# Two-token rows of q and k, Sinkhorn routing on POOL, and weight scales from sums of absolutes, in a one-core attention and expert kernel

## The chip, the cores and the metric

The kernel runs on one core of one Trainium2 chip. The metric is device microseconds of one execution. The engines are PE (matrix products), ACT, DVE and POOL (elementwise work), and SP, which here only issues DMA transfers. Each engine takes its instructions strictly in the order in which they are written for it, and waits where an operand isn't ready.

## The reference

Chunked attention with 8 memory keys is followed by a dense mixture of 8 experts, whose gates are found with 8 Sinkhorn iterations over all 3,072 tokens:

```python
# attention: q, k, v are (4, 8 heads, 768, 64); chunk 32, 16 tokens of left and 8 of right context
k_full = concatenate([mem_k, k_ctx]); v_full = concatenate([mem_v, v_ctx])
scores = scale * q_c @ k_full.T
a = exp(scores - scores.max(-1)); a = a / (a.sum(-1) + 1e-9)
x = a @ v_full                              # reshaped to (3072, 512)
# experts: w_gate (512, 8), w1 (8, 512, 1024), w2 (8, 1024, 512)
logits = x @ w_gate; P = exp(logits - logits.max())
for _ in range(8):
    P /= P.sum(1, keepdims=True) + 1e-9
    P /= P.sum(0, keepdims=True) + 1e-9
    P *= N / E
out = sum(P[:, e:e+1] * (maximum(x @ w1[e], 0) @ w2[e]) for e in range(8))
```

## The kernel before

**Tiling.** Attention goes by 24 blocks of 128 tokens (4 batches of 6). For a block, q and k are loaded with a token on each partition (128 x 8 heads x 64), each of their four 128x128 pieces is turned by PE (`transposed`, tiles tq and tk; for the extra context keys tx), ACT copies the results out (qT, kC), PE makes the scores (sp), DVE takes the row maximum off (sm, s), ACT takes the exponential in place, PE turns it (ta), ACT copies it (at), PE multiplies with v (xp), and DVE divides by the row sums into a tile xq (`share`) and turns it into xg, the layout that the experts read (`turn_out`). xq shares its one buffer with at.

The experts go by 48 units: 8 experts x 6 groups of 512 tokens. Every f32 operand is split into two f16 parts (ACT writes the high part, DVE the low one), and a product is three f16 products. Later units use Strassen's scheme of seven half-size products (px, py, pz for the hidden layer; yx, yy, yz for the output); the very first unit uses plain products (pp, yp). Before a split, a power of two is found for the whole tensor: a maximum of absolutes per partition (`most`, into mxs, or vmax for v, which bounds x), one small maximum over those (most_of), a PE transpose to one row (row_x, row_w), a maximum of that row, a PE product with ones that spreads it (sp_x, sp_w), and a reciprocal (sx, sw).

**Stages.** The attention of later blocks runs among the products of expert 0 (to some 294 us); from some 375 us the rest is a steady row of units. In the prologue PE can do only attention of the first blocks; what it lacks is filled with dummy products called warm (`fill`). The first real product is pp_0_0_0, which needs x of blocks 0 and 1 and the first piece of w1.

**What sets the order.** One planner, `Plan.run`, simulates all engines with a cost for each task and due times (`prio`), and writes the order of each engine's instructions from that; START, TURN, UNIT, AHEAD, BLOCKS, VALUES, FIRST and `needed` feed the due times. Buffers are rings: a task that names a buffer waits for all users of the slot's earlier content. DMA transfers are issued by SP in one stream, except v of the first blocks, which ACT issues.

**Routing.** `routing` runs once, after the last attention block: in each of 8 iterations DVE makes row sums, divides, and makes column sums over its 24 token groups, PE adds over partitions with a product with ones (cp), and DVE scales the columns. Its result, pscale, is first read by an ACT line (`fetch_acc`).

Of the kernel before, what the change touches and what calls it, by code (L numbers as in the profile page):

```python
# [233 lines left out]
def tile_chunked_attn_sinkhorn_moe(  # L234
# [58 lines left out]
    small = ctx.enter_context(tc.tile_pool(name="small", bufs=1))  # L293
    xpool = ctx.enter_context(tc.tile_pool(name="xpool", bufs=1))
# [51 lines left out]
    START, TURN, UNIT, AHEAD = 28.2, 63.0, 36.7, 50.0  # L346
# [340 lines left out]
    def plain1(fp, st, ld, prio):  # L687

        o = operands("w1", [P, 2, 7, 2, P], f"w1_0_{fp}")
# [56 lines left out]
    extra = {}
# [86 lines left out]

    def load_block(n):
# [4 lines left out]
        qt = buf("q", att, [P, H, D], F32, f"q_{n}")  # L839
        kt = buf("k", att, [P, H, D], F32, f"k_{n}")  # L840

        def go_k():
            if blk == 0:
# [5 lines left out]
        lq = add(  # L849
            "SP", 1, lambda: nc.sync.dma_start(qt.t, rows(q, b, t0, QB)), (), at, [qt], dma=1.55  # L850
        )
        lk = add("SP", 2 if blk == 0 else 1, go_k, (), at + 0.1, [kt], dma=1.55)
# [142 lines left out]
    def transposed(n):  # L995
# [10 lines left out]
        def go_q():  # L1006
            for i in range(HP):
                nc.tensor.transpose(tq.t[:, i], flat(qt, i), ident)  # L1008

        def go_k():  # L1010
            for i in range(HP):
# [19 lines left out]
        t = add("PE", 0.5, go_q, [lq], at, [qt, qT], takes=tq)  # L1031
# [11 lines left out]
        t = add("PE", 0.5, go_k, [lk], at, [kt, kC], takes=tk)  # L1043
# [70 lines left out]
    def values(n, s, made):  # L1114
# [31 lines left out]
        t = add("PE", 0.5, go_t, [made], at, [s, aT], takes=tp)  # L1146
# [3 lines left out]
        xq = buf("at", att, [P, CB, KT, CH], F32, f"xq_{n}")  # L1150
        rec = buf("sm", att, [P, H], F32, f"rec_{n}")

        def share():
# [4 lines left out]
            for a in range(2):  # L1158
                nc.vector.tensor_tensor(
                    xq.t[:, :, :, a * CH // 2 : (a + 1) * CH // 2],  # L1160
# [5 lines left out]
        t = add("DVE", 1.25, share, [t], at + 2, [xq, rec], frees=xp)  # L1166
# [11 lines left out]
        def turn_out():  # L1178
            nc.vector.transpose(
                gt.t[:, :, o : o + QB].rearrange("p k (c q) -> p k c q", c=CB),  # L1180
                xq.t.rearrange("p c k f -> p k c f"),
            )

        t = add("DVE", 0.73, turn_out, [t], at + 2, [xq, gt])
# [272 lines left out]

    def routing(deps):
# [4 lines left out]
        urgent = begin(LATE) + 58.5  # L1463
# [27 lines left out]
        def rows(it):  # L1491
            def go():
                rs = small.tile([P, NT], F32, tag="rs", bufs=1, name=f"rs_{it}")
                nc.vector.tensor_reduce(rs, lg, axis=AX.X, op=ALU.add)
                nc.vector.tensor_scalar_add(rs, rs, 1e-9)
                nc.vector.reciprocal(rs, rs)
                nc.vector.tensor_tensor(
                    lg, lg, rs[:, :, None].broadcast_to([P, NT, E]), op=ALU.mult
                )
# [7 lines left out]
        def columns(it, cp):  # L1507
            def go():
                cr = small.tile([P, E], F32, tag="cr", bufs=1, name=f"cr_{it}")
                nc.vector.tensor_scalar_add(cr, cp.t, 1e-9)  # L1510
                nc.vector.reciprocal(cr, cr)
# [811 lines left out]
```

## Time and profile before

| | us |
|---|---|
| median of 3 runs (range) | 1913.08 (1911.89 to 1914.97) |
| the profiled execution: time, span | 1913.3, 1911.5 |
| PE busy, DVE, ACT, POOL | 1898.8, 1468.1, 1022.5, 503.0 |
| granted TensorE clock, mean | 0.999 |

Of PE's busy time, 26.5 us are the 183 dummy products of line 427. Times in the views of the trace count from the first instruction of the span. In a row of the timeline stand the start, the time of the instruction or of the group (a PE group's last matmul is drawn longer than the distance to the next, so start-to-start distances are the better price), the engine, the line, the operation, and in brackets the idle time before it with what ended it. One plain fp32 product shows as two records; a transpose shows as one.

### The profile page before, as it was taken

Reading aid. Unit: us, or ns where it says so; the run is one execution under the profiler, and the core shown is the slowest. Engines: PE = TensorE matmul, PEld = TensorE weight load, DVE = VectorE, ACT = ScalarE, POOL = GpSimd, SP = SyncE. Lnnn points to the kernel's source line nnn. Section 1 sums busy time; section 2 is a strip of 40 time slices with the busy share of each in tenths; the row PEclk is TensorE's granted clock in tenths of the full one; section 3 lists DMA queues with packets and bytes.
Section 4 is the critical chain, followed back from the end, with each engine's and each line's share of the span. In section 5 each row is a group of like instructions: output and inputs, shape, how many; then the busy total and the mean of one; then the engine's idle time right before and its main releaser. Section 6 shows DMA issues by size and latency. Waiting matters only on the chain.

```text
span 1911.5 us, 47024 instructions
## 1 busy us (share of the span) xinstructions
PE 1898.8 (99%) x19535; PEld 1634.8 (86%) x19535; DVE 1468.1 (77%) x2456; ACT 1022.5 (53%) x1999; POOL 503.0 (26%) x541
## 2 busy tenths in 40 slices
PE   8999999999999999999999999999999999999999
PEld 7777676788888888888888888888888888888888
DVE  5887679878589867898668875898678885786565
ACT  4665555556465545546446544655555563564453
POOL 1210012514134211522224231342124232332112
PEclk9999999999999999999999999999999999999999
DMA  8787653543324432264224433245313632222321
GB/s 198 189 219 182 160 173 133 169 169 106 126 80 160 150 134 77 90 217 165 84 91 154 165 119 114 84 155 188 127 45 111 247 112 97 98 84 83 127 84 67
DMA packets 212998, 254.81 MB, mean 133 GB/s; under 512 B 112240, under 2 KB 146480, under 8 KB 208432
## 3 DMA queue, kind: packets, MB, share of 16 engines
q1 hardware_dynamic: 210660, 251.21, 40.4%
q8 instruction: 153, 2.51, 0.6%
q10 hardware_dynamic: 2124, 0.59, 0.2%
q14 instruction: 61, 0.50, 0.1%
HBM read 187.84 MB, written 63.44 MB: 131 GB/s over the span
## 4 chain that ended last, share of the span: by engine, by line
PE 97%; DVE 2%; SPq 0%; ACT 0%; issue 0%; DMA 0%; POOL 0%; DVEq 0%; POOLq 0%
PE px L1593 26%; PE yx L1593 23%; PE pz L1593 13%; PE yz L1593 11%; PE py L1593 6%; PE yp L2121 6%; PE yy L1593 6%; PE pp L2040 1%; PE xp L1138 1%; PE sp L1071 1%; PE warm L427 1%; DVE w L521 1%; PE ta L1128 1%; PE tk L1012 1%; PE tq L1008 1%; SPq L923 0%
## 5 line engine op out<-in xcount | busy, mean ns | idle before, releaser
L1593 PEld LDWEIGHTS <-w 128*128 128x128 f16 x7896 | 771.2, 98 | 94.4 <-issue 2.8
L1593 PEld LDWEIGHTS <-h 128*128 128x128 f16 x7056 | 690.4, 98 | 81.1 <-issue 0.9
L1593 PE MATMUL px<-x,w 128*128 128x256 f16 x4512 | 547.8, 273 | 1.5 <-DVE c L1662 1.0
L1926 POOL TENSOR_TENSOR acc<-acc,y 128x256 f32<-128x256 f32 x252 | 262.4, 1049 | 881.1 <-ACT y L1901 868.5
L1593 PE MATMUL yx<-w,h 128*128 128x256 f16 x4032 | 467.9, 273 | 0.5 <-DVE acc L1936 0.5
L1652 ACT ACTIVATE q<-px 128x256 f32<-128x256 f32 x376 | 143.1, 382 | 289.6 <-PE px L1593 285.1
L1593 PE MATMUL pz<-x,w 128*128 128x256 f16 x2256 | 278.1, 273 | 0.0
L1593 PE MATMUL yz<-w,h 128*128 128x256 f16 x2016 | 233.8, 273 | 0.0
L1821 DVE TENSOR_TENSOR h<-ss,h 128x1024 f16<-128x1024 f32 x168 | 217.6, 1298 | 3.3 <-ACT h L1797 3.3
L1772 ACT ACTIVATE h<-c 128x768 f16<-128x768 f32 x168 | 140.7, 838 | 112.2 <-DVE c L1662 112.2
L1797 ACT CAST h<-ss 128x1024 f16<-128x1024 f32 x168 | 174.2, 1040 | 39.5 <-DVE ss L1761 39.5
L1761 DVE SCALAR_TENSOR_TENSOR ss<-c,ss 128x256 f32<-128x256 f32 x336 | 176.6, 525 | 8.6
L1805 DVE SCALAR_TENSOR_TENSOR h<-c,h 128x768 f16<-128x768 f32 x168 | 168.7, 1007 | 9.2 <-ACT h L1772 9.1
L1662 DVE SCALAR_TENSOR_TENSOR c<-px,q 128x256 f32<-128x256 f32 x188 | 77.8, 421 | 94.8 <-PE px L1593 85.6
L1901 ACT ACTIVATE y<-yx,pscale 128x256 f32<-128x256 f32 x168 | 79.6, 474 | 120.5 <-PE yx L1593 116.5
L1593 PE MATMUL py<-x,w 128*128 128x256 f16 x1128 | 139.0, 273 | 0.0
L2121 PE MATMUL yp<-w,h 128*128 128x512 f16 x576 | 132.0, 379 | 0.9 <-DVE h L2082 0.9
L1761 DVE SCALAR_TENSOR_TENSOR ss<-c,h 128x512 f32<-128x512 f32 x168 | 125.6, 748 | 1.9 <-ACT h L1749 1.9
L1662 DVE SCALAR_TENSOR_TENSOR c<-py,q 128x256 f32<-128x256 f32 x188 | 78.5, 421 | 62.0 <-PE py L1593 58.7
L1593 PE MATMUL yy<-w,h 128*128 128x256 f16 x1008 | 116.9, 273 | 0.0
L2121 PEld LDWEIGHTS <-h 128*128 128x128 f16 x576 | 55.3, 99 | 60.0 <-DVE h L2082 1.4
L513 ACT ACTIVATE w<-ws,sw 128x1024 f16<-128x1024 f32 (+1 forms) x64 | 69.5, 1090 | 65.7 <-POOL ws L601 65.6
(155 smaller groups left out, 1739.6 us busy)
## 6 DMA issues: line engine op xcount, KB each, us to landing
x<-xkeep SPq DMA_DIRECT2D x28, 1792.0 KB
akeep<-acc SPq DMA_DIRECT2D x168, 256.0 KB
acc<-akeep SPq DMA_DIRECT2D x168, 256.0 KB
w1f<-in_moe_w_dram SPq DMA_DIRECT2D x36, 512.0 KB
w2f<-in_moe_w_dram SPq DMA_DIRECT2D x32, 512.0 KB
w1fm<-in_moe_w_dram SPq DMA_DIRECT2D x28, 512.0 KB
w2fm<-in_moe_w_dram SPq DMA_DIRECT2D x28, 512.0 KB
xkeep<-x SPq DMA_DIRECT2D x6, 1792.0 KB
```

Of the source, the lines that this page charges most:

```text
L513: lambda: nc.scalar.activation(dst(0), src(), AF.Copy, scale=s),
L1593: nc.tensor.matmul(dst.t, a, b, start=(not more and n == 0), stop=(n == end), skip_group_check=more,)
L1652: lambda: nc.scalar.activation(t.t, src.t, AF.Copy, scale=DOWN),
L1662: lambda: nc.vector.scalar_tensor_tensor(c.t[:, o], src.t, DOWN, q.t, op0=ALU.mult, op1=ALU.add),
L1761: lambda: nc.vector.scalar_tensor_tensor(dst(), src(), 0.0, other(), op0=ALU.max, op1=op),
L1772: lambda: nc.scalar.activation(h.t[:, 0, 0:3], c.t, AF.Relu),
L1797: lambda: nc.scalar.copy(h.t[:, 0, 3:7], ss.t),
L1805: lambda: nc.vector.scalar_tensor_tensor(h.t[:, 1, 0:3].rearrange("p a n -> p (a n)"), c.t.rearrange("p a n -> p (a n)"), 0.0, h.t[:, 0, 0 ...
L1821: lambda: spare.tensor_tensor(h.t[:, 1, 3:7], ss.t, h.t[:, 0, 3:7], op=ALU.subtract),
L1901: (lambda: nc.scalar.activation(t.t, src.t, AF.Copy, scale=f))
L1926: lambda: nc.gpsimd.tensor_tensor(acc.t[:, cols], acc.t[:, cols], q.t, op=ALU.add),
L2121: nc.tensor.matmul(py.t, hf.t[:, hl, where[fh], o : o + P], room(fp, WIDE * wl + DM * fh, WIDE * wl + DM * (fh + 1)), start=(fp == 0 and i ...
```

## The change

1. **Two-token rows.** For blocks 0 to 5 (`TWOS`), q and k are loaded with two consecutive tokens on one partition row: 64 partitions x 8 heads x 128 elements, so a contiguous run has 512 bytes, not 256. The two buffers of the ring are the two halves of the partitions (0 to 63, 64 to 127) of one tile. PE turns such a tile with 16 plain fp32 products of 64x64 with the identity instead of 4 transposes of 128x128. Later blocks are as before; block 6 waits until block 5 has been turned.
2. **Weight scales from sums.** For w1 of expert 0 and for w1 and w2 of experts 1 to 7 (60 pieces), ACT takes the absolute with a running sum over the partition (`total`, `total_m`) instead of DVE's maximum. w2 of expert 0 keeps the maximum.
3. **Divided results** go into s, the buffer of the softmax weights, instead of xq; at is alone in its buffer.
4. **Fewer waits on PE**: the tasks that turn q, k and s no longer name the buffer into which ACT copies their result.
5. **Routing on POOL**: row sums, the two multiplications and the column sums over groups are POOL additions and products in halves (10 instructions an iteration, into a new tile, tree); DVE adds 1e-9, takes reciprocals and scales 24 or 8 numbers; PE's cp stays. Its due time is earlier, and that of its DVE and PE parts far earlier.
6. **Numbers** of the order: START, TURN, AHEAD, BLOCKS, VALUES, FIRST, `needed`, and the due times of weights, maxima and `rebuild`.

```diff
-    START, TURN, UNIT, AHEAD = 28.2, 63.0, 36.7, 50.0
+    START, TURN, UNIT, AHEAD = 27.4, 66.0, 36.7, 49.9
...
+    def total(fp, which, st, deps, prio, junk):
+        def go():
+            flat = st.t.rearrange("p a k f -> p (a k f)" if which == 1 else "p a d -> p (a d)")
+            nc.scalar.activation(
+                junk.t[:, :, 4:6].rearrange("p j o k f -> p j (o k f)"),
+                flat.rearrange("p (j f) -> p j f", j=2),
+                AF.Abs,
+                accum_out=mxs[:, 0, which - 1, fp : fp + 1],
+            )
+        return add("ACT", 1.15, go, deps, prio, [st, junk])
+    def total_m(e, fp, which, st, deps, prio):
+        def go():
+            flat = st.t.rearrange("p a k f -> p (a k f)" if which == 1 else "p a d -> p (a d)")
+            nc.scalar.activation(
+                flat, flat, AF.Abs, accum_out=mxs[:, e, which - 1, fp : fp + 1]
+            )
+        return add("ACT", 1.1, go, deps, prio, [st])
...
-                found.append(most(e, fp, which, st, [ld], prio))
+                found.append(total_m(e, fp, which, st, [ld], prio))
...
+    TWOS = 6
+    HB = QB // 2
+    qk_rooms = {kind: att.tile([P, 2 * H * D], F32, name=f"{kind}_room") for kind in "qk"}
...
+    def twos(src, b, t, m):
+        return src[b, :, t : t + m].rearrange("h (p a) d -> p h (a d)", a=2)
+    def two_turns(to, t, n):
+        r = slice(n % 2 * HB, (n % 2 + 1) * HB)
+        for i in range(HP):
+            for a in range(2):
+                for par in range(2):
+                    nc.tensor.matmul(
+                        to.t[par * D : (par + 1) * D, i, a::2],
+                        t.t[:, 2 * i + par, a * D : (a + 1) * D],
+                        ident[r, r],
+                        start=True,
+                        stop=True,
+                    )
...
-        t = add("PE", 0.5, go_q, [lq], at, [qt, qT], takes=tq)
+        t = done_q[n] = add("PE", 0.85 if n < TWOS else 0.5, go_q, [lq], at, [qt], takes=tq)
...
-        t = add("PE", 0.5, go_t, [made], at, [s, aT], takes=tp)
+        t = add("PE", 0.5, go_t, [made], at, [s], takes=tp)
...
-        xq = buf("at", att, [P, CB, KT, CH], F32, f"xq_{n}")
+        def turning():
+            return s.t.rearrange("p h k -> p (h k)").rearrange(
+                "p (c k f) -> p c k f", c=CB, k=KT
+            )
...
-        t = add("DVE", 1.25, share, [t], at + 2, [xq, rec], frees=xp)
+        t = add("DVE", 1.25, share, [t], at + 2, [s, rec], frees=xp)
...
-        urgent = begin(LATE) + 58.5
+        urgent = begin(LATE) + 30.0
...
+        def row_sums():
+            two = tree[0][:, 0 : NT * E // 2].rearrange("p (t e) -> p t e", t=NT)
+            one = tree[0][:, NT * E // 2 :].rearrange("p (t e) -> p t e", t=NT)
+            plus(two, lg[:, :, 0 : E // 2], lg[:, :, E // 2 :])
+            plus(one, two[:, :, 0:2], two[:, :, 2:4])
+            plus(rs, one[:, :, 0], one[:, :, 1])
...
         for it in range(8):
-            t = add("DVE", 1.8, rows(it), [t], urgent)
+            t = add("POOL", 1.0, row_sums, [t, opened[0]], urgent)
+            t = add("DVE", 0.5, row_parts, [t], urgent - 300.0)
+            t = add("POOL", 2.1, over_rows, [t], urgent)
...
-            t = add("DVE", 0.8, columns(it, cp), [t], urgent, frees=cp)
+            t = add("DVE", 0.5, column_parts(cp), [t], urgent - 300.0, frees=cp)
+            t = add("POOL", 0.8, over_columns, [t], urgent)
...
-                weights(0, fp, 1, begin(1) - 16.8 + 2.0 * fp)
-            maxima(1, begin(3) + 15.8)
+                weights(0, fp, 1, begin(1) - 10.0 + 2.0 * fp)
+            maxima(1, begin(3) + 0.0)
...
-                weights(e + 1, fp, 1, begin(n + 1) - 8.9 + (0, 0, 20.0, 24.0)[fp])
+                weights(e + 1, fp, 1, begin(n + 1) - -12.9 + (0, 0, 20.0, 24.0)[fp])
```

**DVE, from block 1's scores to the first split of a weight.** Before (mxs: maxima of w1's four pieces; rec, xq, xg: the division and turn of block 1):

```order
L1091 TENSOR_TENSOR s_474<-sp_431,sm_471 128x2x4x64
L976 TENSOR_REDUCE vmax<-v_pair 128x1
L557 TENSOR_REDUCE mxs<-w1f_0_286 128x1
L557 TENSOR_REDUCE mxs<-w1f_1_289 128x1
L1156 TENSOR_SCALAR rec_555<-xp_517 128x8
L1157 RECIPROCAL rec_555<-rec_555 128x8
L1159 TENSOR_TENSOR xq_558<-xp_517,rec_555 128x16x16 x2
L1179 STREAM_TRANSPOSE xg_466<-xq_558 128x4x128
L557 TENSOR_REDUCE mxs<-w1f_2_339 128x1
L557 TENSOR_REDUCE mxs<-w1f_3_363 128x1
L445 TENSOR_REDUCE most_of<-vmax 128x1
L445 TENSOR_REDUCE most_of<-mxs 128x1
```

With the change, from x's scale on:

```order
L458 RECIPROCAL sx<-ux 128x1
L1233 TENSOR_SCALAR rec_588<-xp_552 128x8
L1234 RECIPROCAL rec_588<-rec_588 128x8
L1236 TENSOR_TENSOR s_497<-xp_552,rec_588 128x16x16 x2
L1256 STREAM_TRANSPOSE xg_528<-s_497 128x4x128
L446 TENSOR_REDUCE most_of<-mxs 128x1
L522 SCALAR_TENSOR_TENSOR x_640<-xg_528,sx,x_640 128x512 x2
L503 TENSOR_REDUCE most_of<-row_w_0_649 1x1
...
L458 RECIPROCAL sw<-uw 128x1
L1044 TENSOR_REDUCE vmax<-w_0_2_349 128x1
L522 SCALAR_TENSOR_TENSOR w_0_0_499<-w1f_0_294,sw,w_0_0_499 128x512 x2
```

The four maxima of w1 are gone, x's scale is done before block 1's division, and x's low parts are made before w1's scale; vmax of block 2 (from w_0_2, its buffer) still stands between w1's scale and the first weight split.

**ACT at the same place.** With the change, where before the copy of block 1's at was followed at once by qT of block 2:

```order
L587 ACTIVATE w_0_0_499,mxs<-w1f_0_294 128x2x512
L1182 ACTIVATE s_497<-s_497 128x512
L587 ACTIVATE w_0_1_530,mxs<-w1f_1_298 128x2x512
L1219 COPY at_539<-ta_523 128x512
L587 ACTIVATE w_0_2_585,mxs<-w1f_2_346 128x2x512
L587 ACTIVATE w_0_3_598,mxs<-w1f_3_380 128x2x512
L514 ACTIVATE x_640<-xg_528,sx 128x512 x2
L1108 ACTIVATE qT_668<-tq_623 128x512
```

The four sums stand among block 1's exponential and copy. On PE, 177 of the 183 dummy products stand ahead of the first real product before, and all of 109 now; block 2's scores and the turns of block 3's q and k, which followed the first real product's first half, now stand ahead of it.

**POOL in routing**, one iteration and its neighbours (ws_1_0: the sums of expert 1's first weight piece for Strassen's scheme; tree, row_parts, column_parts: routing):

```order
L625 TENSOR_TENSOR ws_1_0_5553<-w1f_0_5490 128x256
L1609 TENSOR_TENSOR lg<-lg,column_parts 128x192
L1574 TENSOR_TENSOR tree<-lg 128x96
L1574 TENSOR_TENSOR tree<-tree 128x48
L1574 TENSOR_TENSOR row_parts<-tree 128x24
L625 TENSOR_TENSOR ws_1_0_5553<-ws_1_0_5553,w1f_0_5490 128x256
L1588 TENSOR_TENSOR lg<-lg,row_parts 128x192
L1574 TENSOR_TENSOR tree<-lg 128x96
L1574 TENSOR_TENSOR tree<-tree 128x48
L1574 TENSOR_TENSOR tree<-tree 128x24
L1574 TENSOR_TENSOR tree<-tree 128x8 x2
L625 TENSOR_TENSOR ws_1_0_5553<-w1f_0_5490 128x256
```

Before, POOL had only such weight and x sums there, and none of routing. Now 21 of them (of x's last group and of expert 1's weights) stand among the 80 instructions of the 8 iterations.

More of the change, by code (lines that the diff above doesn't have):

```diff
@@ L832, in flat, with qk_buf, make @@
         return t.t[r, 2 * i : 2 * i + 2].rearrange("p h d -> p (h d)")
+    TWOS = 6
+    HB = QB // 2
+    qk_rooms = {kind: att.tile([P, 2 * H * D], F32, name=f"{kind}_room") for kind in "qk"}
+    def qk_buf(kind, n):
+        room_ = qk_rooms[kind]
+        def make(i):
+            if n < TWOS:
+                return room_[i * HB : (i + 1) * HB].rearrange("p (h d) -> p h d", h=H)
+            return room_[:, i * H * D : (i + 1) * H * D].rearrange("p (h d) -> p h d", h=H)
+        return rings[kind].take(make)
+    def twos(src, b, t, m):
[12 more added lines that the diff above has]
+                    )
     def load_block(n):
@@ L838, in load_block, with go_q @@
         at = needed(n) - 25.0 if n >= BU else BLOCKS[n]
-        qt = buf("q", att, [P, H, D], F32, f"q_{n}")
-        kt = buf("k", att, [P, H, D], F32, f"k_{n}")
-        def go_k():
-            if blk == 0:
+        qt = qk_buf("q", n)
+        kt = qk_buf("k", n)
+        out_q = [done_q[n - 1]] if n == TWOS else []
+        out_k = [done_k[n - 1]] if n == TWOS else []
+        cost = 1.1 if n < TWOS else 1.55
+        def go_q():
+            nc.sync.dma_start(qt.t, twos(q, b, t0, QB) if n < TWOS else rows(q, b, t0, QB))
+        def go_k():
+            if n < TWOS:
+                if blk == 0:
+                    nc.sync.dma_start(kt.t[0 : LC // 2], twos(k, b, 0, LC))
+                    nc.sync.dma_start(kt.t[LC // 2 :], twos(k, b, 0, P - LC))
+                else:
+                    nc.sync.dma_start(kt.t, twos(k, b, t0 - LC, P))
+            elif blk == 0:
                 nc.sync.dma_start(kt.t[0:LC], rows(k, b, 0, LC))
@@ L847, in go_k @@
                 nc.sync.dma_start(kt.t, rows(k, b, t0 - LC, P))
[L849 to L852, printed above, removed]
+        lq = add("SP", 1, go_q, out_q, at, [qt], dma=cost)
+        lk = add("SP", 2 if blk == 0 else 1, go_k, out_k, at + 0.1, [kt], dma=cost)
         state[n] = (qt, kt, lq, lk)
@@ L1456, in attention @@
         values(*pend.pop(0))
+    halves_at = small.tile([P, 2, NT], F32, name="row_parts")
+    cols_at = small.tile([P, E], F32, name="column_parts")
     def routing(deps):
@@ L1507, in columns @@
[L1507 to L1511, printed above, removed]
-                nc.vector.scalar_tensor_tensor(
-                    lg,
-                    lg,
-                    float(N) / float(E),
-                    cr[:, None, :].broadcast_to([P, NT, E]),
-                    op0=ALU.mult,
-                    op1=ALU.mult,
-                )
-            return go
+        rs, rr = halves_at[:, 0], halves_at[:, 1]
@@ L1527, in routing @@
                 "PE",
-                0.4,
-                lambda it=it, cp=cp: nc.tensor.matmul(
-                    cp.t, ones, box[it], start=True, stop=True
+                0.2,
+                lambda cp=cp: nc.tensor.matmul(
+                    cp.t,
+                    ones,
+                    tree[0][:, 4 * E : 5 * E],
+                    start=True,
+                    stop=True,
                 ),
                 [t],
-                urgent,
+                urgent - 300.0,
                 takes=cp,
             )
-            t = add("DVE", 0.8, columns(it, cp), [t], urgent, frees=cp)
+            t = add("DVE", 0.5, column_parts(cp), [t], urgent - 300.0, frees=cp)
+            t = add("POOL", 0.8, over_columns, [t], urgent)
         def finish():
@@ L2168, in fetch_first @@
             staged.append((st, ld))
-            found.append(most(0, fp, which, st, [ld], at - 12.0))
+            if which == 1:
+                found.append(total(fp, which, st, [ld], at - 12.0, first1[fp]))
+            else:
+                found.append(most(0, fp, which, st, [ld], at - 12.0))
         scale_w(0, which, found, at - 10.0, "att")
         return staged
+    first1 = [operands("w1", [P, 2, 7, 2, P], f"w1_0_{fp}") for fp in range(FP)]
     first2.extend(operands("w2", [P, 2, 7, DH], f"w2_0_{fp}") for fp in range(FP))
-    for fp, s in enumerate(fetch_first(1, START)):
+    for fp, s in enumerate(fetch_first(1, START + 2.3)):
         plain1(fp, *s, START - 6.0 + 2.0 * fp)
```

69 lines of the change are left out of this document (45 added, 24 removed).

## The prediction

> **What bounds the kernel now.** First the chain of waits of the page, then the busy time by stage:
>
> ```profile
> PE 97%; DVE 2%; SPq 0%; ACT 0%; issue 0%; DMA 0%; POOL 0%; DVEq 0%; POOLq 0%
> ...
> 0.00:38.40 38.40, 33.59 (x480) 26.73 (x481) 18.32 (x40) 13.45 (x26) 4.96 (x12) 0.96 0.80 175
> 38.40:72.00 33.60, 31.86 (x608) 23.71 (x606) 32.29 (x57) 24.72 (x49) 7.32 (x6) 1.00 0.73 179
> ...
> 375.00:1911.00 1536.00, 1531.67 (x14018) 1371.25 (x14015) 1177.82 (x1891) 812.02 (x1581) 432.44 (x453) 1.00 0.35 123
> ```
>
> PE is the bound: after the length of a window stands its busy time, 1531.67 of 1536 in the steady stage. So only two things can move the end: work added to or taken from PE, and PE time that does no work of the problem. The second lies at the start, where dummies fill PE (the same windows for the dummies alone, then the first real product in the timeline):
>
> ```profile
> 0.00:38.50 38.50, 25.70 (x177) 0.96 0.80 175
> 38.50:294.00 255.50, 0.85 (x7) 1.00 0.70 186
> ...
> 38.37 0.82 PE L2040 MATMUL pp<-x,w 128*128 128x256 f16 x6
> ```
>
> Until the first real product at 38.4 us PE has 25.7 us of dummies. Its other large waits, up to 72 us and then behind (in all, times, longest):
>
> ```profile
> PE xp L1138 <- DMA k<-in_k_dram: 1.5, 1, 1.5
> PE yp L2121 <- DVE h L2082: 0.9, 1, 0.9
> PE tk L1012 <- DVE lg L1425: 0.7, 1, 0.7
> ...
> PE px L1593 <- DVE c L1662: 1.0, 3, 0.5
> ```
>
> Behind 38.4 us PE idles 1.7 (33.60 - 31.86) and, from 375 us on, 4.3 us in all. What holds the first product is DVE's chain, told by these rows:
>
> ```profile
> 21.75 0.69 DVE L1091 TENSOR_TENSOR s<-sp,sm 128x512 f32<-128x512 f32 x1
> 23.49 2.33 DVE L557 TENSOR_REDUCE mxs<-w1f 128x1 f32<-128x1024 f32 x2
> 27.10 0.17 DVE L1156 TENSOR_SCALAR rec<-xp 128x8 f32<-128x8 f32 x1 [1.27 <-PE xp L1138]
> 29.03 2.30 DVE L557 TENSOR_REDUCE mxs<-w1f 128x1 f32<-128x1024 f32 x2
> 31.37 0.16 DVE L445 TENSOR_REDUCE most_of<-mxs 128x1 f32<-128x4 f32 x1
> 34.83 0.17 DVE L457 RECIPROCAL sw<-uw 128x1 f32<-128x1 f32 x1
> 35.24 1.22 DVE L976 TENSOR_REDUCE vmax<-w 128x1 f32<-128x1024 f32 x1 [0.24 <-DMA w<-in_v_dram]
> 36.38 1.41 DVE L521 SCALAR_TENSOR_TENSOR x<-xg,sx,x 128x512 f16<-128x512 f32 x2
> 37.70 5.38 DVE L521 SCALAR_TENSOR_TENSOR w<-w1f,sw,w 128x512 f16<-128x512 f32 x8
> ```
>
> Block 1's division (27.10) separates w1's maxima; the last pair ends at 31.3, w1's scale at 35.0, and x's low parts and block 2's vmax (2.6 us together) still stand ahead of the first weight split.
>
> **The change part by part.** *The first product.* The transfers that the new order leans on:
>
> ```profile
> 18.66 0.55 SPq L850 DMA_DIRECT2D q<-in_q_dram  x1
> 19.31 3.53 SPq L847 DMA_DIRECT2D k<-in_k_dram  x1
> 22.93 7.54 SPq L923 DMA_DIRECT2D w<-in_v_dram  x8
> 30.57 0.39 SPq L850 DMA_DIRECT2D q<-in_q_dram  x1
> 31.06 0.54 SPq L847 DMA_DIRECT2D k<-in_k_dram  x1
> ...
> DMA packets 2047, 0.52 MB, mean 258 GB/s; under 512 B 2047, under 2 KB 2047, under 8 KB 2047
> ...
> DMA packets 638, 0.63 MB, mean 315 GB/s; under 512 B 23, under 2 KB 638, under 8 KB 638
> ...
> 22.48 0.63 ACT L1110 ACTIVATE s<-s 128x512 f32<-128x512 f32 x1 [1.97 <-DVE s L1091]
> 34.40 1.33 ACT L513 ACTIVATE x<-xg,sx 128x512 f16<-128x512 f32 x2 [0.19 <-DVE sx L457]
> ```
>
> The packets are those of 12 to 14 us (256-byte q, k) and of 20 to 22 us (1 KB, w1). Runs of 512 bytes have no row; between the two rates 256 KB take 0.83 to 1.02 us, so 0.1 is saved a transfer by bytes. By count it is more: SP is held for 3.5 us at k of block 2 and block 2's v pieces take 7.5 us for 8 issues, with 2,048 packets of q and k ahead; half as many should free about 2 us of it. I take v of block 2 landed by 29 to 30, k of block 3 by some 32.
>
> The DVE chain, step by step. Block 1's maximum and subtraction now precede block 0's division, so s ends near 20.8 (22.4 before); exponential, ta, its copy and xp follow as before with 4.6 us from s to the division (27.10 - 22.44), less 1.5 of a wait for a transfer inside: division at 24.0 to 24.6, turn out (1.9 us, 27.10 to 29.03) at 26.5. ACT's sums have no row; the nearest, ACT's 128x1024 cast, is
>
> ```profile
> L1797 ACT CAST h<-ss 128x1024 f16<-128x1024 f32 x168 | 174.2, 1040 | 39.5 <-DVE ss L1761 39.5
> ```
>
> 1.04 us, so 1.1 each (lower 1.0; upper 1.4, two 0.7 us halves, as ACT's 128x512 rows have it). The last two fall at 24 to 26.6, behind at and w1's landing. Then most_of at 26.8; x's parts on ACT 26.6 to 28.0 and DVE to 28.7; row_w meanwhile on PE; its maximum, the power of two, sp_w and sw: now 3.6 (31.37 to 35.0) with x's own scale and a wait for row_x inside, a third of it without them, 1.2: 29.9; vmax 1.2: 31.1; first split 0.7: 31.8. PE's list, however, has sp of block 2 (0.8), three dummies and both turns of block 3 ahead of the product, some 3.1 us behind sw: 33.0, and 33.3 with k of block 3 landing at 32. Product at 33.3 instead of 38.4: **-5.1**. Bounds: 31.8 (DVE alone) to 36.5 (below).
>
> *PE work brought forward and made dearer:*
>
> ```profile
> 55.66 0.86 PE L1071 MATMUL sp<-kC,qT 64*32 64x64 f32 x64
> 48.23 0.60 PE L1012 MATMUL tk<-ident,k 128*128 128x128 f32 x4
> 48.67 0.82 PE L2040 MATMUL pp<-x,w 128*128 128x256 f16 x6
> 63.43 1.08 PE L1394 MATMUL lp<-xg,gate 128*32 128x128 f32 x32
> 64.44 1.47 PE L2121 MATMUL yp<-w,h 128*128 128x512 f16 x6
> ```
>
> Block 2's scores (0.79) and block 3's two turns (0.44 each, 48.23 to 48.67) no longer follow the first product: **-1.7**. The 16 products of 64x64 have no row. Nearest is lp: 16 plain fp32 products with 128 columns moved and a quarter of the array's columns used take 1.01, 63 ns each; half the columns moved and twice the array's columns make the same, so 1.0 us for 16. Below, sp's 25 ns a product: 16 in 0.4, no dearer than now. Above, if the halves of the array don't overlap: 2.0. I take 1.0, +0.56 a turn. Blocks 0 to 3 pay it in dummy time (that is in the 33.3); blocks 4 and 5, four turns, pay it on PE: **+2.2** (0 to +6.2).
>
> *Sums of later weights.* DVE loses 60 times 1.2 us, ACT gains 60 times 1.1. Both hide behind PE, DVE being the fuller (1177.8 against 812.0 of 1536). Cover gone would cost at most what a read of PSUM delayed by 1.1 us costs at a piece, and px waits for DVE's c already for 1.0 in all; I take **-0.5** for all waits behind 38.4 us (from -2.7 to +3). The first output product waits for the low part of h, that is for DVE:
>
> ```profile
> 67.86 1.21 DVE L2082 SCALAR_TENSOR_TENSOR h<-c,h 128x512 f16<-128x512 f32 x1
> ```
>
> From the first weight split (37.70) to its end are 31.4 us, DVE without pause. The new order puts 1.4 us more ahead of it (block 4's maximum and subtraction): from a split at 32.6, 65.4, 3.7 earlier than now. PE has by then six more products of yp and one more turn behind it (1.3 + 0.4), so the gain by this chain is 5.4, against 5.1 - 2.2 + 1.7 = 4.6 by PE's own list: neither chain takes back what the other gives.
>
> *Routing.*
>
> ```profile
> L1497 DVE TENSOR_TENSOR lg<-lg,rs x8: 357/358/511, 300.7 to 331.8; 128x192 f32<-128x192 f32 x8
> ...
> 300.27 0.73 POOL L601 TENSOR_TENSOR ws<-w1f 128x256 f32<-128x256 f32 x1 [5.74 <-DMA w1f<-in_moe_w_dram]
> 340.42 1.17 POOL L601 TENSOR_TENSOR ws<-w1f,ws 128x256 f32<-128x256 f32 x1
> ...
> 373.08 0.70 ACT L1852 ACTIVATE acc<-acc,pscale 128x512 f32<-128x512 f32 x1
> ```
>
> POOL takes 0.73 for 256 elements; with 0.1 of fixed time assumed, one iteration's ten (two of 192, two of 96, two of 48, two of 24, two of 8) are 2.8 us. DVE's five small ones, at the 0.17 of the row at 27.10, are 0.9, cp and the hand-overs 0.5. The 21 weight and x sums among them are 18 at 0.85. All told 8 x 4.2 + 18 = 52 us; it ends before 350, and its reader is at 373. cp stands in PE's list with 60 to 72 products between two, at 109 ns (1531.67 by 14018, above) 59 us for the eight: no wait, **0**. The buffer of s for xq and the dropped names: **0**, hidden in the order above.
>
> Sum: 1913.3 (the profiled execution, 0.2 above the median) - 5.1 - 1.7 + 2.2 - 0.5 = 1908.2; by the median **1908.0**.
>
> **Rivals.** *A, rows of two tokens don't come sooner.* A transfer that fills 64 partitions may be no faster than one of 128. Then SP's stops stay, k of block 3 is issued until 31.6, it and q are 512 KB or 2.0 us at 258 GB/s, I allow as much again for the way, and the product stands behind its turn (1.0) at 36.5: -1.9 - 1.7 + 2.2 - 0.5: 1911.1. [...] No transfer of 64 full partitions is in this trace. For A: only the partition count speaks; against it: the packet rows, where size alone sets the rate.
>
> *B, the halves of the array run one after the other:* 2.0 a turn, product at 35.3: -3.1 - 1.7 + 6.2 - 0.5 = +0.9: 1913.9. For it: nothing in the trace uses two halves of 64 columns; against: sp and lp do overlap.
>
> *C, slower: PE waits at cp.* If POOL's small additions take 0.35 each, whatever their width, an iteration is 3.5 + 0.9 + 1.0, and with sums at 1.17 (the row at 340.42) the eight are 43 + 25 = 68 us against 59 on PE. It decides from 7.4 us an iteration on: PE, in order, loses the 9 us: +3.9, 1917.0. For it: POOL's row varies from 0.73 to 1.17 for the same work where DVE is full; against: the row at 300.27, inside the routing of now, has 0.73.
>
> *D, the covers hold everywhere:* turns at 0.6, product at 32.2, later waits -2: -6.2 - 1.7 + 0.6 - 2 = 1904.0.
>
> **How the numbers follow.** Forecast 0.50 (its own range 1904.8 to 1911), A 0.15, B 0.10, C 0.13, D 0.12. A measurement tells 0.2%, 3.8 us, from no change: faster is below 1909.3. Faster: 0.43 of the forecast, 0.03 of A, all of D: 0.58. Slower, above 1916.9: 0.01 of the forecast, 0.03 of B, 0.11 of C: 0.15. Same: 0.27. The range leaves out D's lower half and C's upper half: 1902.5 to 1915.5.
>
> **What would show it.** Fewer dummies (109) and the first pp at 32 to 34.5 show the first step; a pp behind a tk that waits for a transfer shows A. The distance of 16 products of 64x64 shows their price: 1.0, and 2.0 is B. A wait of PE at cp shows C. Gaps of PE at expert starts larger than 0.5 would show that ACT's sums delay PSUM reads. The forecast is wrong if the first pp comes early and the yp rows give it back to DVE: a wait over 3 us ahead of them.

## The result

The changed kernel is slower by 0.7%: 1925.42 us median of 5 runs (1922.29 to 1927.62) against 1913.08, a ratio of 1.0066, 95% interval 1.0052 to 1.008. One further run of the kernel before took 2449.49 us and isn't in the ratio. The prediction had said 1908.0, 1902.5 to 1915.5, and faster. The profiled execution is the fastest of the five, 1922.29 us with a span of 1920.5, 9.0 above the span before; the profile explains these 9 and not the other 3.3 between the medians. The other runs have no trace, but their mean granted clock is on record: 0.995 in the two longest (1927.49 and 1927.62), 0.998 and 0.999 in the rest. By an estimate from these figures, 0.003 of the clock over 1922 us are 5.8 us, and the two longest lie 5.3 above the profiled one. So these two fit the clock; where in the run it was lost isn't shown.

### The profile page after: what moved, and what is told of

The parts are those of the page before. It is cut to its first block, busy times and chain, and to the rows that moved or that the text cites. A ratio compares the mean times of both kernels' runs of the same rounds, so it can differ in the third digit from the quotient of the medians.

```text
span 1920.5 us, 47672 instructions
## 1 busy us (share of the span) xinstructions
PE 1900.7 (99%) x19797; PEld 1635.1 (85%) x19797; DVE 1392.7 (73%) x2372; ACT 1081.9 (56%) x2119; POOL 535.3 (28%) x621
## 4 chain that ended last, share of the span: by engine, by line
PE 91%; DVE 3%; POOL 2%; DMA 2%; SPq 1%; ACT 1%; issue 1%; DVEq 0%; POOLq 0%; ACTq 0%
PE px L1690 24%; PE yx L1690 23%; PE pz L1690 12%; PE yz L1690 11%; PE py L1690 6%; PE yy L1690 6%; PE yp L2218 5%; POOL tree L1574 1%; DVE ss L1858 1%; PE xp L1210 1%; PE sp L1143 1%; DMA k_room<-in_k_dram 1%; SPq L991 1%; PE warm L428 1%; DMA w2f<-in_moe_w_dram 1%
## 5 line engine op out<-in xcount | busy, mean ns | idle before, releaser
L1918 DVE TENSOR_TENSOR h<-ss,h 128x1024 f16<-128x1024 f32 x168 | 225.1, 1343 | 3.3 <-ACT h L1894 3.3
L1858 DVE SCALAR_TENSOR_TENSOR ss<-c,ss 128x256 f32<-128x256 f32 x336 | 168.0, 500 | 8.1
L2218 PEld LDWEIGHTS <-h 128*128 128x128 f16 x576 | 55.4, 98 | 58.8 <-issue 0.2
L522 DVE SCALAR_TENSOR_TENSOR w<-ws,sw,w 128x1024 f16<-128x1024 f32 (+1 forms) x64 | 80.2, 1255 | 34.3 <-ACT w L514 34.3
```

The costliest lines, as they stand in the source:

```text
L522: lambda: nc.vector.scalar_tensor_tensor(dst(1), src(), s, dst(0), op0=ALU.mult, op1=ALU.subtract),
L1858: lambda: nc.vector.scalar_tensor_tensor(dst(), src(), 0.0, other(), op0=ALU.max, op1=op),
L1918: lambda: spare.tensor_tensor(h.t[:, 1, 3:7], ss.t, h.t[:, 0, 3:7], op=ALU.subtract),
L2218: nc.tensor.matmul(py.t, hf.t[:, hl, where[fh], o : o + P], room(fp, WIDE * wl + DM * fh, WIDE * wl + DM * (fh + 1)), start=(fp == 0 and i ...
```

## The profile after

The chain of waits, which was PE 97% before, and the busy time by the same stages (after the length stands PE's busy time, then PEld, DVE, ACT, POOL, the clock, the DMA share and GB/s):

```profile
PE 91%; DVE 3%; POOL 2%; DMA 2%; SPq 1%; ACT 1%; issue 1%; DVEq 0%; POOLq 0%; ACTq 0%
...
38.40:72.00 33.60, 30.43 (x626) 23.11 (x623) 25.88 (x46) 20.39 (x39) 6.49 (x5) 0.96 0.68 163
...
294.00:375.00 81.00, 74.48 (x515) 49.79 (x514) 61.75 (x117) 42.78 (x78) 62.41 (x103) 1.00 0.33 107
375.00:1911.00 1536.00, 1534.65 (x14014) 1371.01 (x14012) 1131.28 (x1846) 865.07 (x1687) 430.15 (x461) 1.00 0.36 124
```

PE, which was busy for all 81.0 us of the stage from 294 to 375 before, lost 6.5 there, and POOL went from 26.83 to 62.41. Between 38.4 and 72 it lost 3.2 (33.60 - 30.43), with the clock below 1. In the steady stage PE loses nothing (1534.65 busy of 1536; the same window of before had 1531.67, with the end of the program in it). PE's waits up to 72 us and from 290 on:

```profile
PE tq L1078 <- DMA q_room<-in_q_dram: 1.9, 1, 1.9
PE tq L884 <- DMA q_room<-in_q_dram: 1.7, 2, 1.3
...
PE tk L884 <- DMA k_room<-in_k_dram: 0.8, 1, 0.8
...
PE cp L1621 <- POOL tree L1574: 6.5, 7, 1.7
```

Waits of the turns for transfers of q and k, and the waits at cp for POOL's sums, are new; before, the one such wait of PE up to 72 us was 1.5 us at an xp. First and last start of yx, one kind of product of the Strassen units, tell what is left in the end (kernel before, changed, and the first experiment below):

```profile
L1593 PE MATMUL yx<-w,h x4032: 269/273/273, 392.0 to 1908.1; 128*128 128x256 f16 x192
```

```profile
L1690 PE MATMUL yx<-w,h x4032: 272/273/273, 402.0 to 1916.8; 128*128 128x256 f16 x192
```

```profile
L1670 PE MATMUL yx<-w,h x4032: 272/273/273, 393.4 to 1908.2; 128*128 128x256 f16 x192
```

The lag is made before 392 us: 10.0 there, of which 1.3 comes back. The first real product starts at 38.05 (38.37 before), the first output product yp at 62.0 (59.4), so the prologue's gain of 0.3 is a loss of 2.6 by then. Around the first real product, on PE, and the granted clock (the figure behind the five engines):

```profile
34.44 1.97 PE L884 MATMUL tq<-ident,q_room 64*64 64x64 f32 x32 [1.28 <-DMA q_room<-in_q_dram]
36.20 1.92 PE L884 MATMUL tk<-ident,k_room 64*64 64x64 f32 x32
38.05 7.64 PE L2137 MATMUL pp<-x,w 128*128 128x256 f16 x54
```

```profile
34.00:36.00 2.00, 1.56 (x30) 1.56 (x32) 2.00 (x5) 2.00 (x4) 0.00 (x0) 0.62 1.26 161
36.00:38.00 2.00, 2.00 (x40) 1.93 (x38) 2.00 (x5) 0.84 (x2) 0.00 (x0) 0.50 0.73 98
38.00:40.00 2.00, 2.00 (x14) 1.40 (x11) 1.97 (x4) 0.00 (x0) 0.00 (x0) 0.50 0.66 144
40.00:42.00 2.00, 2.00 (x14) 1.56 (x13) 0.69 (x1) 1.17 (x3) 0.00 (x0) 0.68 0.97 365
```

Block 3's turns, which the new order puts ahead of the first product, wait 1.28 us for their transfer. Then the clock is at half until 41 us: the two turns take 1.8 us each (34.44 to 36.20 to 38.05) and the products run at half speed (pp starts every 0.21 us until 41.2, every 0.11 from 41.4 on). By the clock column 0.76 + 1.0 + 1.0 + 0.64 = 3.4 us of full-speed work are lost in these 8 us, at most, since PE stood still for the first 0.4.

## The experiments

In the table the median and the ratio are of the timed runs, the ratio to runs of the kernel before taken beside them (medians 1913.79 to 1914.51 for the experiments); the last four columns are of the one profiled execution. That one can stand anywhere among its kernel's runs: dve_route's is the fastest of ten, that of sums_alone the slowest. The prologue varies too: where only routing was changed (pool_alone), the first product started at 36.5 and not at 38.4. So differences below 2 us there are read only where a wait or a clock names them.

| kernel | median | ratio, 95% interval | first pp | first yp | first yx | waits at cp |
|---|---|---|---|---|---|---|
| before | 1913.08 | | 38.4 | 59.4 | 392.0 | none |
| changed | 1925.42 | 1.0066 (1.0052 to 1.0080) | 38.0 | 62.0 | 402.0 | 6.5 |
| dve_route | 1915.70 | 1.0010 (1.0001 to 1.0020) | 36.9 | 61.3 | 393.4 | none |
| late_cp | 1917.60 | 1.0021 (1.0012 to 1.0030) | 37.5 | 63.1 | 395.9 | 0.2 |
| pool_alone | 1920.65 | 1.0035 (1.0022 to 1.0048) | 36.5 | 58.8 | 399.9 | 5.1 |
| twos_alone | 1923.98 | 1.0049 (1.0032 to 1.0065) | 39.2 | 62.6 | 402.8 | none |
| sums_alone | 1914.91 | 1.0005 (0.9996 to 1.0015) | 31.9 | 56.0 | 396.1 | none |
| sums_early | 1915.24 | 1.0008 (0.9999 to 1.0018) | 35.3 | 56.2 | 392.8 | none |
| one_token | 1926.17 | 1.0064 (1.0049 to 1.0079) | 33.1 | 58.2 | 406.2 | 6.9 |
| one_dve | 1919.31 | 1.0025 (1.0015 to 1.0035) | 32.9 | 56.1 | 396.5 | none |
| same_order | 1921.02 | 1.0031 (1.0017 to 1.0046) | 36.3 | 57.6 | 400.7 | 6.5 |
| same_order_dve | 1911.76 | 0.9992 (0.9983 to 1.0001) | 36.8 | 59.2 | 393.4 | none |
| dummies | 1923.92 | 1.0062 (1.0046 to 1.0079) | 37.1 | 60.3 | 403.5 | 6.4 |
| best | 1914.77 | 1.0008 (0.9999 to 1.0017) | 36.1 | 57.2 | 392.7 | none |

### Routing: what the waits at cp cost

The theory from the two traces: PE takes cp in its place in the order, and POOL isn't done by then (6.5 us of waits, at seven of the eight). Two undo it in different ways: dve_route gives the eight iterations back to DVE, with their former due time; late_cp keeps them on POOL and only tells the planner higher costs.

```diff
-            t = add("POOL", 1.0, row_sums, [t, opened[0]], urgent)
+            t = add("POOL", 1.7, row_sums, [t, opened[0]], urgent)
...
-            t = add("POOL", 2.1, over_rows, [t], urgent)
+            t = add("POOL", 3.2, over_rows, [t], urgent)
...
-            t = add("POOL", 0.8, over_columns, [t], urgent)
+            t = add("POOL", 1.1, over_columns, [t], urgent)
```

> The changed kernel with routing back on DVE, everything else of the change kept. Theory (PE, in order, waits at the eight cp for POOL's sums: 6.5 us of gaps in the trace, and the lag to the kernel before grows by 7.3 us between 300 and 365 us): no wait ahead of any cp, about 7 us less than the changed kernel, 1915 to 1919 by runs, still 2 to 3 slower than the kernel before. Rival (the gaps at cp only show elsewhere what another part delays, ACT's sums or the new due times): the time stays within 2 us of the changed kernel and PE's gaps between 290 and 365 us appear at px or yp instead.

> The changed kernel; only the costs by which the order is written are raised for the three POOL steps of an iteration (from 1.0, 2.1, 0.8 to 1.7, 3.2, 1.1, near the 1.5, 2.7, 1.0 that their records take), so each cp stands later in PE's list, some 90 products behind the one before instead of 67. Theory (the wait comes from an order written for a faster POOL, not from POOL's use itself): cp waits fall below 1 us in all, 5 to 7 us less than the changed kernel. Rival (POOL is late by whatever the order gives it, or what reads the routing result now waits): 0 to 2 us less.

Both went the way of the theory, and further: 9.7 and 7.8 us off the changed kernel's median, where some 7 and 5 to 7 were expected (8.9 and 6.1 by the spans of the profiled executions). Late_cp's waits from 290 us on have this left of the 6.5:

```profile
PE cp L1621 <- POOL tree L1574: 0.2, 1, 0.2
```

So the waits came from where cp stood, not from POOL doing the work. The third looks at the part alone: the kernel before with only routing moved to POOL, with the change's due times.

> The kernel before with one part of the change alone: routing on POOL, with its due times and costs. Theory (the wait at cp is a price of this part, whatever the others do): cp waits of 5 to 8 us in all between 290 and 365 us, 1919 to 1922. Rival (the waits in the changed kernel came of the late start of routing or of ACT's and DVE's other new work): cp waits below 2 us, within 3 us of the kernel before.

It is 6.1 us slower than the kernel before in its own runs (1914.51), with this wait:

```profile
PE cp L1545 <- POOL tree L1498: 5.1, 7, 1.4
```

Why POOL was late stands in the groups of the changed kernel (busy in all, mean ns; 8 or 16 instructions each) and in two rows of its timeline:

```profile
L1574 POOL TENSOR_TENSOR tree<-lg 128x96 f32<-128x96 f32 x16 | 9.9, 618 | 28.0 <-ACT lg L1569 26.8
L1574 POOL TENSOR_TENSOR tree<-tree 128x48 f32<-128x48 f32 x16 | 9.1, 570 | 1.3
L1609 POOL TENSOR_TENSOR lg<-lg,column_parts 128x192 f32<-128x192 f32 x8 | 7.7, 962 | 1.8 <-PE px L1690 1.5
L1574 POOL TENSOR_TENSOR tree<-tree 128x8 f32<-128x8 f32 x16 | 4.6, 290 | 1.3
L1588 POOL TENSOR_TENSOR lg<-lg,row_parts 128x192 f32<-128x192 f32 x8 | 4.6, 573 | 4.1 <-DVE row_parts L1585 4.1
L1574 POOL TENSOR_TENSOR tree<-tree 128x24 f32<-128x24 f32 x8 | 3.2, 401 | 0.6
L1574 POOL TENSOR_TENSOR row_parts<-tree 128x24 f32<-128x24 f32 x8 | 2.8, 344 | 0.6
```

```profile
291.54 0.39 POOL L1574 TENSOR_TENSOR tree<-lg 128x96 f32<-128x96 f32 x1 [26.79 <-ACT lg L1569]
...
293.81 1.25 POOL L1574 TENSOR_TENSOR tree<-lg 128x96 f32<-128x96 f32 x1
```

They add up to 41.9 us, 5.2 an iteration, where the prediction had 2.8. Eight numbers take 0.29 and not 0.12, and the same sum of 96 numbers took 0.39 once and 1.25 two us later. What lengthened it wasn't tested. With the 21 weight and x sums among them and the waits for DVE, POOL's part of routing lasted 67.7 us (291.54 to 359.26), where the prediction had 52 for the whole and its rival C 68.

### Two-token rows: turns and transfers

The kernel before with this part alone:

> The kernel before with one part of the change alone: two-token rows of q and k for blocks 0 to 5. Theory (16 products take 1.09 us against 0.44 for a turn, six turns of blocks 3 to 5 stand behind the first product, and the transfers land no sooner): 3 to 5 us slower, 1916 to 1918; the first product within 1.5 us of 38.4. Rival (half the packets free the queue): q of block 2 turned 1 us or more before 31.5, the first product 2 us earlier, within 1 us of the kernel before in all.

The direction was right, the size not: 9.5 us slower in its runs. By the first output product the lag is 3.2 (62.6 by 59.4), as expected; the other 7.6 come later, with a wait of 3.2 at a turn of k's extra rows for a transfer, and new dummies, in an order that the planner wrote anew. So the part can't be priced with the order moving. The same shows in the opposite try, the changed kernel with one-token rows throughout (`TWOS = 0`), and with routing back on DVE as well:

> The changed kernel with q and k of all blocks in one-token rows, turned by four transposes as in the kernel before. Theory (a turn by 16 products costs 1.09 us against 0.44, and four of them lie on PE's path: 2.6 us; the packets of 512 bytes took 53 ns between 24 and 32 us, so the two-token transfers weren't sooner): about 2 to 3 us less than the changed kernel at the first output product and in all, and q of block 3 lands no later. Rival (two-token rows do free the queue): q and k of block 3 land 1 us or more later, the first real product behind 38.4, the total within 1 us of the changed kernel.

> The changed kernel without its two dear parts: one-token rows for all blocks, and routing on DVE; sums on ACT, divided results in s, dropped names and due times kept. Theory (turns by products and cp waits are the whole loss, the rest gains): no cp wait, first product near 33, 2 to 5 us faster than the kernel before, 1908 to 1912. Rival (the prologue's gain is given back by waits for transfers and for DVE before 300 us, as with one-token rows alone, where the first product came 5 us sooner and the lag at 250 us was +1.5): within 2 us of the kernel before, 1912 to 1916.

The first product came at 33, near the prediction's 33.3, yet one_token's median did not fall (1926.17) and one_dve's stayed 4.8 above the kernel before. Both expectations were missed: 38 of the dummies moved behind the first product, and in one_dve PE waited 3.8 us at 375 us for a weight of expert 1. Both change the planner's costs, and with them the whole order. So the next pair holds the order: the planner sees the changed costs, and only what is issued for blocks 0 to 5 differs.

```diff
-            nc.sync.dma_start(qt.t, twos(q, b, t0, QB) if n < TWOS else rows(q, b, t0, QB))
+            nc.sync.dma_start(qt.t, rows(q, b, t0, QB))
...
-            if n < TWOS:
-                return two_turns(tq, qt, n)
```

> The changed kernel with the order of every engine's work as the change has it, but q and k of blocks 0 to 5 are loaded in one-token rows and turned by four transposes (in place of 16 products). Theory (the two-token rows cost their turns, 0.65 us each, and bring no earlier landing): the first product 1 to 2 us earlier than 38.05, four turns behind it save 2.6, so the lag at the first output products falls from 2.65 to about -1 and the total by 3 to 4 us, 1921 to 1922.5, cp waits unchanged. Rival (the transfers do land sooner with 512-byte runs): the turn of block 3's q waits longer than 1.3 us, and the total falls by less than 1.5.

> As the run before, with routing back on DVE as well. Theory (the two dear parts removed without moving the rest of the order): 2.5 to 4 us less than with routing back on DVE alone (1915.7 beside 1914.2 of the kernel before), 1911.5 to 1913, faster than the kernel before by 1 to 3. Rival (an earlier PE meets later waits for DVE, ACT or transfers, as the sums alone did): 1914 to 1916.

By the medians these came out as the theory said: 4.4 us less than the changed kernel, and 3.9 less than dve_route (1911.76). The traces show it only at the start. The first output product comes 4.4 and 2.1 us sooner, but the first yx only 1.3 sooner and no sooner (400.7 for 402.0, 393.4 for 393.4). In same_order's trace the next turn of q waits longer than in the changed kernel (1.9 there), the clock falls for 3.4 us behind that wait, and PE stops for 1.2 us at 175 us:

```profile
63.11 1.11 PE L1068 MATMUL tq<-ident,q_room 128*128 128x128 f32 x4 [2.79 <-DMA q_room<-in_q_dram]
```

So the two-token rows are dear at the start by both measures; how much of it lasts is read from the medians alone. Of the 4.4 at the first output product the turns are 3.9: by 16 products they took 1.09 us each on PE at full clock (47.45 to 48.54 for block 4) against 0.44 to 0.49, 2.6 for the four behind the first product, and from the start of block 3's first turn to the first product it is 3.6 against 2.3. The other 0.5 is the transfer. Block 3's q and k, in the same place of SP's order, first two views of the changed kernel (SP's issue; what DMA moved from 33 to 34 us), then three with one-token rows (SP's issue; PE's turn; DMA again):

```profile
29.55 1.48 SPq L904 DMA_DIRECT2D q_room<-in_q_dram  x1
```

```profile
DMA packets 413, 0.21 MB, mean 208 GB/s; under 512 B 8, under 2 KB 413, under 8 KB 413
```

```profile
30.54 0.39 SPq L902 DMA_DIRECT2D q_room<-in_q_dram  x1
```

```profile
33.97 0.66 PE L1068 MATMUL tq<-ident,q_room 128*128 128x128 f32 x4 [1.99 <-DMA q_room<-in_q_dram]
```

```profile
DMA packets 1035, 0.26 MB, mean 261 GB/s; under 512 B 1035, under 2 KB 1035, under 8 KB 1035
```

SP began to issue the two-token q 1.0 us sooner, was done with it 0.1 later (31.03 against 30.93), and it was ready 0.5 later (34.44 against 33.97). Fewer, larger packets moved fewer bytes in this microsecond: 208 against 261 GB/s; over the two from 32 to 34 us it is 223 against 244. That is one pair of windows; what sets the rate inside DMA wasn't taken apart.

### Sums on ACT: an early start that doesn't last

The kernel before with this part alone, and then with all due times behind the prologue 5 us earlier (`START` 23.2):

> The kernel before with one part of the change alone: the 60 maxima of weights as ACT's sums. Theory (the earlier first product of the changed order comes from this part: DVE loses 4.7 us of maxima ahead of it): first product at 33 to 35 instead of 38.4; part of it is given back at the first output products, where DVE and transfers are late; 1909 to 1912. Rival (ACT's 1.25 us each, with the read of the sum, delay its reads of PSUM at each expert's start): gaps of PE there grow, 1914 or more.

> The kernel before with ACT's sums alone, and every due time behind the prologue 5 us earlier (START 23.2 in place of 28.2). Theory (the first product's 6.4 us are given back because transfers of q and the splits of x are still due for the later start): the waits for q's transfers (4.1 us) and x's splits (3.5) halve, the lag at 135 us falls from +3.3 to about 0, 1910 to 1913. Rival (DMA and DVE are full between 30 and 110 us whatever is due): the same waits elsewhere, 1914 to 1917.

The sums do start the work early: 31.9 instead of 38.4, the largest gain of any run. It is all given back: no difference can be measured (1.0005, 0.9996 to 1.0015), where 1909 to 1912 was expected. The rival's cause isn't it either: PE's waits behind 290 us are 1.6 us in all, as in the kernel before (1.5). PE's waits from 40 to 175 us in sums_alone, a stretch in which the clock also falls once, for 3.4 us from 114 us on:

```profile
PE tq L1031 <- DMA q<-in_q_dram: 4.1, 3, 2.2
PE px L1616 <- DVE x L521: 2.8, 2, 1.6
PE sp L1094 <- issue: 1.4, 1, 1.4
PE px L1616 <- ACT x L513: 0.7, 1, 0.7
```

With earlier due times the waits for q are gone and those for x's splits fall to 1.5, as the theory said, but more dummies stand in their place, and the first product comes at 35.3 and not at 31.9. By the traces the first yx is 3.3 us sooner (392.8 for 396.1); the median doesn't move (1915.24), as the rival said. So what feeds PE between 40 and 175 us, transfers and DVE's splits, seems to be no earlier than before, and PE meets it sooner. That is argued from these rows: no run made the suppliers earlier with the order held. A sum of its own, from the changed kernel, costs this on ACT:

```profile
24.06 1.06 ACT L587 ACTIVATE w<-w1f 128x1024 f16<-128x1024 f32 x1
25.02 0.18 ACT L587 ACTIVATION_READ_ACCUMULATOR w<-w1f 128x1 f32 x1
```

### The clock

The changed kernel with 14 more dummies ahead of block 3's turn of q:

```diff
+            if n == 3:
+                for _ in range(14):
+                    nc.tensor.matmul(tq.t.rearrange("p h q -> p (h q)")[:, 0:256], idle[:, 0:P], idle, start=True, stop=True)
```

> The changed kernel with 14 more dummy products on PE right ahead of block 3's turn of q, where PE sat idle for 1.3 us for a transfer and the granted clock then read 0.5 to 0.68 until 42 us. Theory (the idle stretch cost the clock, and the clock cost work): clock 1.0 from 34 to 42 us, the first real product within 0.5 us of 36.7 instead of 38.05, and 3 us less at the first output product (62.0), 2 to 3 us less in all. Rival (what follows waits for DVE or transfers anyhow): first product earlier, first output product within 1 us of 62.0, total unchanged.

Granted clock from 34 to 36 and from 38 to 40 us with them:

```profile
34.00:36.00 2.00, 2.00 (x41) 1.71 (x40) 2.00 (x4) 2.00 (x5) 0.00 (x0) 1.00 1.21 160
...
38.00:40.00 2.00, 2.00 (x21) 1.80 (x19) 2.00 (x4) 1.39 (x4) 0.00 (x0) 1.00 0.81 190
```

The first half of the theory holds: 1.00 where 0.62 and 0.50 stood, the first product 1.0 us sooner, the first output product 1.7 (3 was expected). The second half fell: the median is within 1.5 us (1923.92). By the trace the gain is lost at 170 us, where PE stops in the middle of block scores and the clock falls again behind it, for 3.4 us:

```profile
172.56 0.31 PE L1152 MATMUL sp<-kC,qT 64*32 64x64 f32 x5 [1.88 <-issue]
```

```profile
173.05:176.46 3.41, 3.41 (x19) 2.41 (x17) 1.25 (x2) 1.44 (x4) 0.00 (x0) 0.50 0.70 179
```

The stop and half of the 3.4 us are 3.6, and they turn a lead of 2.0 at the last pp (92.2 for 94.2) into a lag of 1.5 at the first yx. In dve_route and late_cp, too, which have the same list of work just ahead of the first product, PE had no wait before block 3's turns and the clock stood at 1.00 from 34 to 42 us: the first product came at 36.9 and 37.5, the first output product only at 61.3 and 63.1, with other waits and another fall (from 58.96 and 47.51 us) in between. So a clock that holds at the first product didn't by itself bring the output products forward.

Not every wait was followed by a lower clock. In the 14 traces each stretch at half clock that isn't cut off by the end lasts 3.41 or 6.83 us. In the changed kernel it is 34.47 to 41.30; here is the 3.41 us ahead of it, and a stretch of the same length from 65.19 us on, with a wait of 1.85 us, that was followed by full clock:

```profile
31.06:34.47 3.41, 1.80 (x72) 1.24 (x71) 1.94 (x4) 2.85 (x7) 0.00 (x0) 1.00 0.84 166
65.19:68.60 3.41, 1.97 (x12) 1.29 (x13) 3.41 (x4) 3.32 (x8) 3.17 (x2) 1.00 0.69 153
```

PE was busy for 0.53 and 0.58 of them. Ahead of 18 of the 19 falls the share was 0.11 to 0.61, ahead of one 0.88 (twos_alone, 14.94 to 18.35 us), and shares from 0.50 up were also followed by full clock (0.50 from 353.95 us on, in the run with dummies). So the share alone doesn't decide, and what else does wasn't tested.

The timed runs show that 14 dummies don't settle the matter: their mean granted clock is 0.998 (0.997 to 0.999), that of the changed kernel's runs 0.997, that of the kernel before, beside the experiments, 0.9995. By an estimate from these, 0.0025 of 1920 us, the clock would be some 5 of the 12 us between the medians.

Last, the version that the rest pointed to: same_order_dve with 22 and 8 dummies ahead of block 3's turns.

> One-token rows and routing on DVE in the order of the change, as in the run before last, with 22 dummy products ahead of block 3's turn of q and 8 ahead of that of k, where PE idled 2.2 and 0.3 us for transfers and the clock then read 0.5 until 40 us. Theory (the clock lost there is work lost): clock 1.0 from 32 to 42 us, the first output product 2 to 3 us earlier than 59.2, and 1 to 3 us less in all than 1911.8, 1909 to 1911, clearly faster than the kernel before. Rival (as with the 14 dummies in the changed kernel, what is won there is given back by later waits for transfers): first output product earlier, total within 1 us of 1911.8.

Neither came out. In the trace the clock held (1.00 from 32 to 42 us), the first output product came 2.0 us sooner than without them, and from 72 us on PE waited for this, where same_order_dve has 1.2 us at one xp:

```profile
PE xp L1216 <- issue: 2.3, 2, 1.9
PE tq L1077 <- issue: 0.6, 1, 0.6
```

By the traces 0.7 us are left of the 2.0 (the first yx at 392.7 for 393.4). Its median is 1914.77, 3.0 above same_order_dve, where the rival had it within 1; the timed runs of both stand at a mean clock of 0.998, so that doesn't explain it, and the cause is open. No version beat the kernel before clear of the measurement; same_order_dve is nearest (0.9992, 0.9983 to 1.0001). It holds parts 3, 4 and 6 of the change together with the sums; none of these three has a run of its own.

## Why the prediction was wrong, step by step

**Routing, "no wait, 0".** This step failed, and it is the largest. POOL's ten instructions were priced from the 128x256 sums by width with 0.1 us of fixed time assumed, 2.8 an iteration; they took 5.2. No addition on POOL shows the 0.1: the shortest in the trace after took 0.20. Rival C had the mechanism (cp in PE's order, decided at 7.4 us an iteration) and a chance of 0.13. The eight cp span 58.5 us in the trace (297.28 to 355.73), 8.4 from one to the next, 6.5 of them waits where C had 9. Shown by three runs: alone it costs 6.1 us, taken back it saves 9.7, and with the work on POOL but cp later 7.8.

**First product, "-5.1".** Measured -0.3. The DVE chain of the prediction ran 1.9 us behind: w1's scale at 31.8 for 29.9, block 2's v landed at 32.85 for 29 to 30, so the first split began at 34.0:

```profile
31.63 0.16 DVE L458 RECIPROCAL sw<-uw 128x1 f32<-128x1 f32 x1
32.85 1.22 DVE L1044 TENSOR_REDUCE vmax<-w 128x1 f32<-128x1024 f32 x1 [1.06 <-DMA w<-in_v_dram]
33.99 5.38 DVE L522 SCALAR_TENSOR_TENSOR w<-w1f,sw,w 128x512 f16<-128x512 f32 x8
```

The failed step is the landing "k of block 3 by some 32", from half the packet count: SP's stops stayed (v of block 2 took 8.75 us to issue, 7.54 before) and q landed at 34.4. That is rival A, whose 36.5 was still short, since neither it nor the forecast had the clock. Without the fall of the clock the product stands at 36.9 to 37.5 (dve_route, the run with dummies, late_cp).

**Turns, 1.0 us each.** Right: 1.09, so +2.6 for the four on PE's path against +2.2. The nearest row, lp, was the right one to take; rival B is out.

**"Neither chain takes back what the other gives".** Wrong in kind. Sums_alone has an early first product of 6.4 us, and its median shows nothing of it. A gain at the first product was entered into the sum as if what comes behind were PE's alone; behind it stand waits for q, for x's splits and stops that the profile names no cause for, and no part of the sum has them.

**All later waits, "-0.5".** This covers all waits behind 38.4 us but those at cp, and up to 72 us alone they grew by 1.5 (3.2 for 1.7). Only from 392 us on was the sign right: there the lag shrinks from 10.0 to 8.7, and PE idles 0.7 less between the first and the last yx (1.07 for 1.73).

With measured terms: first output product +2.6 (first product -0.3, block 3's turns and block 2's scores brought forward -1.7, dearer turns +2.6, the rest the slow clock and waits for transfers), waits at cp +6.5, about 1 more until 392 us that no single row carries, -1.3 from there on: +9, as the spans say. The 3.3 us by which the medians differ more have no term. (Small slips: from 1913.1 the sums of the rivals give 1911.2 for A, 1914.0 for B and 1903.8 for D, where the prediction has 1911.1, 1913.9 and 1904.0; nothing rests on them.)

## What to carry to other kernels

Where an engine takes its work strictly in order, a chain moved to a slower engine must be priced by that engine's small instructions, as they run beside their neighbours, before anything that waits for it is given its place; with a late place PE waited 0.2 us here, with an early one 6.5. Price a part with the order held: in twos_alone, where the order was written anew, 7.6 of the 10.8 us at the first yx came behind the first output product, from waits and dummies elsewhere. And an early start counted for nothing in these runs where the suppliers of the next 100 us were no earlier: look at what PE would wait for next before the gain enters a sum. Last, compare medians and traces: one traced execution can be the fastest or the slowest of its kernel.

## What the runs showed of the hardware

- In the changed kernel a wait of 1.28 us, with an idle stretch of 0.33 that ended 1.1 us ahead of it, was followed by 6.83 us at a clock of 0.50, and with 14 dummies in its place the clock stood at 1.00 from 30 to 46 us; a wait of 1.85 us in the trace of the changed kernel was followed by full clock. In the 3.41 us ahead of the fall PE was busy for 0.53 of the time. In the 14 traces a stretch at half clock lasted 3.41 or 6.83 us, but for those that the end cuts off.
- In one pair of windows of 1 us, DMA moved 208 GB/s with q and k loaded to 64 partitions in 512-byte runs (changed kernel) and 261 with 256-byte runs to 128 partitions (same_order); what sets the rate wasn't tested.
- In the changed kernel's routing POOL's additions on a partition took 0.20 us at the least for 8 numbers and 0.39 for 96, and up to 1.3 for 48 and 96 alike.
- In many of these kernels PE stops, mostly within a run of small products, for 0.2 to 2.0 us at a time, for nothing that the profile names ("issue"). In the run with dummies the stop at 170.7 us stands beside a load of the instruction queue q8 while the transfer queue was full (169 to 173 us):

```profile
q1 hardware_dynamic: 205, 1.70, 102.0%
q8 instruction: 1, 0.02, 1.5%
```

Whether PE waited for its instructions there isn't shown. The run has 155 loads of q8, one in 12 us on average, and one each from 173 to 177 and from 177 to 181 us, with no such stop.
